# Gradients of a GELU layer: copies out of one PSUM tile put in the planned order, and the engines' orders written anew

## The chip, the cores and the metric

One core of one Trainium2 chip. The metric is the device time of one execution in microseconds; the span in the profile goes from the first to the last instruction. Engine names as in the profile: PE is TensorE (PEld its weight loads), DVE VectorE, ACT ScalarE, POOL GpSimd, SP SyncE, which here issues DMAs.

## The reference

A dense layer with tanh-GELU and a second dense layer, forward and backward. All inputs and outputs are bfloat16. S = 2048 rows, D = 448, F = 1792.

```python
h = jnp.einsum("bsd,df->bsf", x, w1) + b1
h = gelu(h)                                   # tanh form
out = jnp.einsum("bsf,fd->bsd", h, w2) + b2
# outputs: out, and the gradients of x, w1, b1, w2, b2 for a given grad_out
```

## The kernel before, in words

Every engine's program is a list written out by hand: `PE_ORDER`, `ACT_ORDER`, `DVE_ORDER`, `SP_ORDER`. A token names a step. A small planner (`Plan`) turns the tokens into operations. `emit` writes an operation out when everything that it needs has been written out, engine by engine in the order of the lists; the semaphores follow from the tiles that the written instructions share. So where two engines use one tile, the one written out first goes first, and the other waits.

The rows are worked in 4 blocks of 512. In each block the 1792 columns of the hidden layer go in 7 pairs of 128-column tiles, so there are 28 pairs, p = 0 to 27. The steps:

- PE: `W6`, `w4` are warm-up matmuls; `X0` to `X3` transpose four tiles of x for block 0; `B` spreads b2. `u p.d` is x times w1 for pair p, in two runs d = 1, 2, of 3 and 4 pairs of matmuls (d = 1 has 4 and d = 2 has 3 for p below 7). A pair of matmuls is two half-height matmuls side by side, into two PSUM banks. `h0.d` and `h1.d` are u for pair 0 in two halves of 256 columns: h0 needs x's tiles 0 and 1, h1 needs tiles 2 and 3. `q p.d` is grad_out times w2 transposed, into the tile `qb` (banks 6 and 7). `p p.i` are the units of the output in block 0, two pairs of matmuls each; `o b.half...` are units of the output of block b and `x b.half...` units of x's gradient, 4 or 6 pairs of matmuls each, into banks 0 to 3. After the last unit stand the gradients of w1 (L780) and of w2 (L834), 16 matmuls for each bank.
- u goes to banks 4 and 5 in general, but to 0 and 1 for p = 1 and to qb's two banks for p = 2 and p = 4 (`U_BANK`). Bank halves change sides between d = 1 and d = 2, and a run waits for a word from POOL (L235) where that is so.
- `c pA`, `c pB` copy u's two banks with b1 into a bf16 tile (L410 on ACT, L412 on DVE). `X0` to `X3` in the lists of ACT and DVE empty x's transposed tiles (L582). `b1T` transposes b1 in four small instructions (L675), and every c needs it. `b2c` empties B's bank.
- ACT: `g` GELU (L430), `s` square (L435), `t` tanh (L460). DVE: `e`, `r`, `y`, `z`, `m`, `n` (L440 to L470) work out the derivative, and `G` (L475) multiplies it with q out of qb. So q of pair p + 1 can start only when G of pair p is done.
- `vo b.j` empties a bank of the output with b2 (L496, always DVE), `vx b.j` a bank of x's gradient (L501 on ACT).
- SP: `L0` to `L3` load parts of w1, `Z0` to `Z2` its last 128 rows into `gh_nat`, `F` and `R` two more copies of 64 rows of w1, `K` parts of w2, `X`, `Y` transposing loads of x and grad_out, `J`, `I` transposed weights, `H`, `T` stores and transpositions of h and its gradient, `S` stores of output blocks, `Nx`, `Ng` loads for the last stage.

u of pair 2 wants L2 and Z1; u of pair 4 wants L3 and, with its fourth pair of matmuls, Z2.

In `C` (L395 on) stands the rule on copies out of qb. It acts only where B is on DVE and A on ACT, and no pair of this kernel is so: c2A is on DVE and c2B on ACT, and both c4 are on DVE.

Of the kernel before, what the change touches and what calls it, by code (L numbers as in the profile page):

```python
# [108 lines left out]
ACT_ORDER = """
xr12 L0 Z0 b2 table X1 X3 c0A0 c0A1 s0 g0 s1 g1 c2B t0 s2 g2 g3 s3 c5B g4 g5 t1 c6B t2 g6 s4 s5 g7 c8A c8B g8 c9A c9B  # L110
g9 c10A c10B t3 t4 g10 s6 c11A c11B s7 g11 t5 c12A c12B g12 s8 t6 c13A c13B g13 s9 t7 s10 c14A c14B t8 t9 g14 c15A s11
s12 c15B t10 g15 c16A s13 c16B t11 g16 vx0.0 vx0.1 s14 c17A c17B t12 vx0.2 vx0.3 g17 s15 c18A c18B t13 g18 s16 c19A
c19B t14 g19 t15 c20A s17 c20B g20 s18 t16 c21A c21B s19 t17 g21 c22A c22B g22 s20 t18 c23A c23B g23 s21 t19 s22 t20
s23 c24A c24B t21 vx1.0 vx1.1 vx1.2 vx1.3 g24 s24 c25A c25B t22 t23 g25 s25 c26A c26B s26 g26 t24 c27A c27B g27 s27
t25 vx2.0 vx2.1 vx2.2 vx2.3 t26 t27 vx3.0 vx3.1 vx3.2 vx3.3
"""
DVE_ORDER = """
ident X0 b1T X2 b2c c0B0 c0B1 c1A c1B e0 r0 y0 c2A c3A c3B z0 e1 m0 r1 n0 c4A c5A c4B z1 e2 y1 r2 y2 z2 c6A m1 n1 m2
n2 c7A c7B Dg0 G0 vo0.2 vo0.3 e3 r3 vo0.0 z3 vo0.1 G1 y3 e4 r4 y4 z4 m3 n3 m4 G2 n4 e5 r5 y5 z5 G3 m5 e6 n5 r6 y6 z6
G4 m6 e7 n6 r7 y7 z7 G5 m7 e8 vo1.0 r8 vo1.1 z8 vo1.2 vo1.3 G6 n7 e9 y8 r9 y9 z9 m8 G7 m9 n8 n9 e10 r10 y10 z10 G8 e11  # L120
m10 r11 n10 z11 y11 G9 m11 e12 n11 r12 y12 z12 G10 m12 e13 n12 r13 y13 z13 G11 e14 r14 m13 z14 n13 y14 G12 e15 r15 y15
m14 z15 n14 m15 G13 n15 e16 r16 y16 z16 G14 m16 e17 n16 r17 y17 z17 vo2.0 vo2.1 G15 m17 vo2.2 vo2.3 n17 e18 r18 y18
z18 G16 m18 e19 n18 r19 y19 z19 m19 G17 n19 e20 r20 y20 z20 G18 m20 e21 n20 r21 y21 z21 G19 e22 r22 m21 z22 n21 y22
G20 e23 r23 y23 z23 m22 n22 m23 G21 n23 e24 r24 y24 z24 m24 n24 G22 e25 r25 y25 z25 m25 G23 n25 e26 r26 y26 z26 m26
G24 n26 e27 r27 y27 z27 m27 n27 G25 vo3.0 vo3.1 G26 vo3.2 vo3.3 G27
"""
# [33 lines left out]
def make_plan(tc, ctx, x, w1, b1, w2, b2, grad_out, out_0, out_1, out_2, out_3, out_4, out_5):  # L160
# [239 lines left out]
    def C(p, h, eng, hf=None):  # L400
        ft = 2 * (p % NPB) + h
        v = val(("ub", p), F_UB[p])
        if hf is None:
# [4 lines left out]
        bias = b1T[:, ft:ft + 1]
        if eng == "ACT":
            fn = lambda: nc.scalar.activation(out=out, in_=src, func=ACT.Identity, bias=bias)  # L410
        else:
            fn = lambda: nc.vector.tensor_scalar(out=out, in0=src, scalar1=bias, scalar2=None, op0=ALU.add)  # L412
# [465 lines left out]
```

## Time and profile before

| | us |
|---|---|
| median of 3 runs | 266.11 (265.84 to 266.29) |
| the profiled execution | 266.0 |
| its span | 264.2 |
| PE busy | 259.6 |
| DVE busy | 196.2 |
| ACT busy | 131.5 |

A row of the timeline gives start, length, engine, line, operation, output from input, count, and in brackets the idle time ahead of it with what ended it. A row of the waits gives the total, the times and the longest. A row of a stage gives its ends, its length, then busy time and count of PE, PEld, DVE, ACT and POOL, the granted clock, the DMA engines' share and GB/s. A matmul's end is modelled, so its start is the firmer number. The granted TensorE clock is 1.00 throughout.

### The profile page before, as it was taken

What the parts mean: (1) busy time and instruction counts of PE and PEld (TensorE: products, weight loads), DVE (VectorE), ACT (ScalarE), POOL (GpSimd) and SP (SyncE); (2) the same over time, 40 slices, a digit from 0 to 9 for tenths busy, and PEclk for the clock granted to TensorE, in tenths of its full rate; (3) what the DMA queues carried; (4) which work ended last, traced back from release to release, by engine and by line L of the source; (5) the groups of instructions that cost most, each with busy time, mean ns of one, the idle gap of its engine ahead of it and who ended that gap; (6) DMA issues with size and microseconds to landing.
All of it is one profiled execution on the core that took longest, in us unless ns stands there. A gap on an engine that the chain in (4) does not pass through costs nothing.

```text
span 264.2 us, 5344 instructions
## 1 busy us (share of the span) xinstructions
PE 259.6 (98%) x2185; PEld 158.2 (60%) x2185; DVE 196.2 (74%) x279; ACT 131.5 (50%) x172; POOL 14.6 (6%) x12
## 2 busy tenths in 40 slices
PE   8989999999999999999999999999999999999996
PEld 4545555566666666677677777765555555555554
DVE  6699399899978899999996986379999996011000
ACT  4789749864889896973998430021112111000001
POOL 1000000000000000000000000000000872100000
PEclk9999999999999999999999999999999999999999
DMA  7999988999997965594557942895898999973221
GB/s 209 298 188 227 168 138 191 285 317 203 252 215 154 212 178 122 136 178 107 102 143 197 298 96 42 149 289 137 176 235 159 163 226 164 226 167 119 69 72 35
DMA packets 120107, 46.50 MB, mean 176 GB/s; under 512 B 96671, under 2 KB 119953, under 8 KB 120082
## 3 DMA queue, kind: packets, MB, share of 16 engines
q1 hardware_dynamic: 119392, 45.71, 79.1%
q10 hardware_dynamic: 690, 0.44, 0.5%
q8 instruction: 17, 0.28, 0.5%
q14 instruction: 8, 0.07, 0.1%
HBM read 8.09 MB, written 14.28 MB: 85 GB/s over the span
## 4 chain that ended last, share of the span: by engine, by line
PE 94%; ACT 2%; DVE 2%; DMA 1%; issue 0%; POOL 0%; DVEq 0%; ACTq 0%; POOLq 0%
PE bank L240 45%; PE qb L240 16%; PE bank L780 16%; PE bank L834 16%; DMA b1n<-in_b_dram 1%; ACT HG L430 1%; ACT TR L435 1%; DVE gh_nat L412 1%; DVE ub L412 0%; DVE b1T L675 0%; DVE xT L582 0%; ACT ub L410 0%; POOL st L667 0%; ACT w_sb L839 0%; POOL b1n L670 0%
## 5 line engine op out<-in xcount | busy, mean ns | idle before, releaser
L240 PEld LDWEIGHTS <-HG 64*128 64x128 bf16 x896 | 60.2, 94 | 27.8 <-POOLq L235 1.9
L240 PE MATMUL qb<-gT,w2Tf 64*128 64x512 bf16 x392 | 53.6, 376 | 0.0
L240 PE MATMUL bank<-w_sb,HG 64*128 64x448 bf16 x448 | 49.0, 349 | 0.0
L240 PE MATMUL bank<-xT,w1f 64*128 64x512 bf16 (+1 forms) x360 | 48.3, 370 | 0.7 <-DVE xT L582 0.4
L240 PE MATMUL bank<-w1T_sb,HG 64*128 64x448 bf16 x448 | 48.3, 349 | 0.0
L475 DVE SCALAR_TENSOR_TENSOR HG<-TR,qb 128x1024 bf16<-128x1024 bf16 x28 | 34.0, 1216 | 13.8 <-PE qb L240 13.8
L834 PE MATMUL bank<-w2Tf,HG 128*128 128x448 bf16 (+2 forms) x240 | 42.6, 340 | 0.0
L780 PE MATMUL bank<-w1f,gh_nat 128*128 128x448 bf16 x224 | 42.5, 352 | 0.0
L240 PEld LDWEIGHTS <-w2Tf 64*128 64x128 bf16 x392 | 26.4, 94 | 14.2 <-POOLq L235 0.3
L834 PEld LDWEIGHTS <-HG 128*128 128x128 bf16 x240 | 22.9, 98 | 19.8
L780 PEld LDWEIGHTS <-gh_nat 128*128 128x128 bf16 x224 | 21.8, 98 | 20.6 <-issue 0.4
L240 PEld LDWEIGHTS <-w1f 64*128 64x128 bf16 x382 | 23.6, 94 | 17.3 <-issue 1.3
L460 ACT ACTIVATE TR<-TR 128x1024 bf16<-128x1024 bf16 x28 | 29.3, 1054 | 8.4 <-DVE TR L450 8.1
L803 DVE TENSOR_TENSOR w1T_sb<-w1T_sb,gh_nat 128x1792 f32<-128x1792 f32 x14 | 28.4, 2026 | 0.5
L840 DVE CAST w_sb<-bank 128x448 bf16<-128x448 f32 x6 | 3.7, 624 | 29.7 <-PE bank L834 29.7
L785 ACT ACTIVATE TR<-bank 128x448 bf16<-128x448 f32 x14 | 7.6, 544 | 34.3 <-PE bank L780 34.3
L839 ACT CAST w_sb<-bank 128x448 bf16<-128x448 f32 (+2 forms) x9 | 4.4, 491 | 37.7 <-PE bank L834 37.7
L465 DVE TENSOR_SCALAR TR<-TR 128x2048 bf16<-128x2048 bf16 x28 | 19.2, 687 | 4.1 <-ACT TR L460 4.1
L809 POOL PARTITION_ALL_REDUCE w1T_sb<-w1T_sb x1 | 10.6, 10570 | 203.7 <-DVE w1T_sb L807 203.7
L470 DVE TENSOR_TENSOR TR<-TR 128x1024 bf16<-128x1024 bf16 x28 | 19.1, 685 | 0.2
L455 DVE TENSOR_TENSOR TR<-TR,HG 128x1024 bf16<-128x1024 bf16 x28 | 19.1, 683 | 0.0
L435 ACT ACTIVATE TR<-gh_nat 128x1024 bf16<-128x1024 bf16 x15 | 15.6, 1049 | 7.0 <-DVE TR L470 6.9
(51 smaller groups left out, 190.5 us busy)
## 6 DMA issues: line engine op xcount, KB each, us to landing
hT_dram<-HG SPq DMA_DIRECT2D x28, 256.0 KB, 3.9
out_dram<-st SPq DMA_DIRECT2D x16, 224.0 KB, 2.7
w1f<-in_x_dram SPq DMA_DIRECT2D x2, 896.0 KB, 8.1
w2Tf<-in_grad_out_dram SPq DMA_DIRECT2D x2, 560.0 KB
...
```

The costliest lines, as they stand in the source:

```text
L240: m = nc.tensor.matmul(bk_(b)[:, 0:n], lhsT=l, rhs=r, start=st, stop=sp, skip_group_check=True)
L435: pl.op("ACT", f"s{p}", lambda: nc.scalar.activation(out=TR[p % NTR][:, 1], in_=ubuf(p), func=ACT.Square, scale=sc), [("ub", p)], [v], ("a ...
L455: pl.op("DVE", f"R{p}", lambda: nc.vector.tensor_tensor(out=t[:, 1], in0=t[:, 1], in1=hblk(p), op=ALU.mult), [("r", p), ("h", p)], [val((" ...
L460: pl.op("ACT", f"t{p}", lambda: nc.scalar.activation(out=t[:, 0], in_=t[:, 0], func=ACT.Tanh), [("y", p)], [val(("t", p), ("TR0", p % NTR) ...
L465: pl.op("DVE", f"m{p}", lambda: nc.vector.tensor_scalar(out=t[:], in0=t[:], scalar1=1.0, scalar2=None, op0=ALU.subtract), [("t", p), ("r2" ...
L470: pl.op("DVE", f"n{p}", lambda: nc.vector.tensor_tensor(out=t[:, 0], in0=t[:, 0], in1=t[:, 1], op=ALU.mult), [("m0", p), ("m1", p)], [val( ...
L475: pl.op("DVE", f"G{p}", lambda: nc.vector.scalar_tensor_tensor(out=ghblk(p), in0=t[:, 0], scalar=2.0, in1=qb[:, :, :], op0=ALU.subtract, o ...
L780: nc.tensor.matmul(bk_(bk)[:, 0:D], lhsT=gh_nat[:, st // 4, ft, st % 4, :], rhs=x_nat[:, st, :], start=(st == 0), stop=(st == NS - 1))
L785: fn = (lambda dst=dst, src=src: nc.scalar.mul(out=dst, in_=src, mul=-0.5)) if eng == "ACT" else \
L803: nc.vector.tensor_tensor(out=hs3, in0=a, in1=gh_nat[:, st // 4, :, st % 4, :], op=ALU.add)
L809: pl.op("POOL", "gb1", lambda: nc.gpsimd.partition_all_reduce(gb1_w, hsum, channels=P, reduce_op=bass_isa.ReduceOp.add), ["hsc"], ["gb1"], ...
L834: nc.tensor.matmul(bk_(bk)[:, 0:d1 - d0], lhsT=h_nat[ft][:, st, :], rhs=g_nat[:, st, d0:d1], start=(st == 0), stop=(st == NS - 1))
```

## The change

One rule is widened and the four orders are written anew. The work is the same: the same matmuls, copies and loads.

```diff
-        if hf is None and u_banks(p)[0] == 6 and f"c{p}B" in DVE_ORDER.split() and f"c{p}A" in ACT_ORDER.split():
-            if eng == ("DVE" if p in ACT_FIRST else "ACT"):
-                after(o, [("u", p, 1 - h)])
+        other = DVE_ORDER if eng == "ACT" else ACT_ORDER
+        if hf is None and u_banks(p)[0] == 6 and f"c{p}{'BA'[h]}" in other.split() and eng == ("DVE" if p in ACT_FIRST else "ACT"):
+            after(o, [("u", p, 1 - h)])
```

`after` makes an operation be written out behind all readers of the named value: c2B on ACT is now written out after c2A on DVE.

The orders, cut to where they differ most:

```diff
 PE_ORDER
-... p0.0 p0.1 p0.2 p0.3 p1.0 u4.1 u5.1 u4.2 u5.2 p1.1
+... p0.0 p0.1 p0.2 p0.3 p1.0 p1.1 u4.1 u5.1 u4.2 u5.2
-... q6.2 x0.0.0.6.1 u14.1 x0.1.0.6.1 u14.2 q7.1 x0.0.0.6.2
-q7.2 u15.1 x0.1.0.6.2 u15.2 q8.1 x0.0.6.10.1 q8.2 x0.1.6.10.1 x0.0.6.10.2 u16.1 x0.1.6.10.2 u16.2 q9.1 x0.0.10.14.1
+... q6.2 x0.0.0.6.1 x0.1.0.6.1 u14.1 q7.1 u14.2 q7.2
+x0.0.0.6.2 x0.1.0.6.2 u15.1 q8.1 u15.2 q8.2 x0.0.6.10.1 x0.1.6.10.1 u16.1 q9.1 u16.2 q9.2 x0.0.6.10.2 u17.1
...
-... q18.1 x1.1.6.10.1 q18.2
-x1.0.6.10.2 x1.1.6.10.2 q19.1 x1.0.10.14.1 q19.2 ...
+... x1.0.0.6.2 q18.1 x1.1.0.6.2 q18.2 x1.0.6.10.1
+x1.1.6.10.1 q19.1 x1.0.6.10.2 q19.2 ...
...
-x2.0.0.6.1 x2.1.0.6.1 q21.1 u26.1 q21.2 u26.2 x2.0.0.6.2 x2.1.0.6.2 u27.1 x2.0.6.10.1 u27.2 x2.1.6.10.1 q22.1
+... q21.1 u26.1 q21.2 u26.2 x2.0.0.6.1 x2.1.0.6.1 x2.0.0.6.2 u27.1 x2.1.0.6.2 u27.2 q22.1 x2.0.6.10.1 q22.2
...
 ACT_ORDER
-... c2B t0 s2 g2 g3 s3 c5B g4 g5 t1 c6B t2 g6 s4 s5 g7 ...
+... c2B t0 s2 g2 g3 s3 c5B g4 t1 t2 c6B g5 g6 s4 s5 g7 ...
-... vx0.0 vx0.1 ... vx0.2 vx0.3 ... vx1.0 vx1.1 vx1.2 vx1.3 ... vx2.0 vx2.1 vx2.2 vx2.3 ... vx3.0 vx3.1 vx3.2 vx3.3
+... vx0.2 ... vx1.1 vx1.3 ... vx2.0 vx2.2 ... vx3.0 vx3.2
 DVE_ORDER
-ident X0 b1T X2 b2c c0B0 c0B1 c1A c1B e0 r0 y0 c2A c3A c3B z0 e1 m0 r1 n0 c4A c5A c4B z1 ...
+ident X0 X2 b1T c0B0 b2c c0B1 c1A c1B e0 r0 y0 c2A c3A c3B z0 e1 m0 r1 n0 z1 c4A c5A c4B ...
+... n12 z13 vx0.0 vx0.1 G11 vx0.3 ... G20 vx1.0 vx1.2 ... n25 vx2.1 vx2.3 ... G27 vx3.1 vx3.3
 SP_ORDER
-xr01 xr24 b1 L1 L2 Z1 K0 L3 K1 Z2 K2 F X1 K3 R Y0 J0 J1 Y1 J2 I0 E J3 I1 ...
+xr01 xr24 b1 L1 Z1 L2 K0 L3 K1 F Z2 K2 X1 K3 R Y0 J0 J1 J2 Y1 I0 E J3 I1 ...
```

The further steps of u, q, o and x, and the stores and transpositions on SP's queue, change places by a few steps in the same manner.

More of the change, by code (lines that the diff above doesn't have):

```diff
@@ L91 @@
 PE_ORDER = """
-W6 X0 X1 w4 X2 X3 h0.1 B h0.2 h1.1 u1.1 h1.2 u1.2 u2.1 u3.1 u2.2 u3.2 p0.0 p0.1 p0.2 p0.3 p1.0 u4.1 u5.1 u4.2 u5.2 p1.1
+W6 X0 X1 w4 X2 X3 h0.1 B h0.2 h1.1 u1.1 h1.2 u1.2 u2.1 u3.1 u2.2 u3.2 p0.0 p0.1 p0.2 p0.3 p1.0 p1.1 u4.1 u5.1 u4.2 u5.2
 p1.2 p1.3 p2.0 p2.1 p2.2 p2.3 u6.1 p3.0 u6.2 p3.1 p3.2 p3.3 p4.0 p4.1 u7.1 p4.2 u7.2 p4.3 p5.0 p5.1 p5.2 p5.3 u8.1
-p6.0 u8.2 q0.1 p6.1 q0.2 u9.1 p6.2 u9.2 q1.1 p6.3 q1.2 u10.1 o1.1.0.6.1 u10.2 q2.1 o1.0.0.6.1 u11.1 q2.2 u11.2
+p6.0 u8.2 q0.1 p6.1 q0.2 u9.1 p6.2 u9.2 q1.1 p6.3 q1.2 u10.1 o1.0.0.6.1 u10.2 q2.1 o1.1.0.6.1 u11.1 q2.2 u11.2
@@ L95 @@
 o1.0.0.6.2 o1.1.0.6.2 q3.1 u12.1 q3.2 u12.2 o1.0.6.10.1 q4.1 o1.1.6.10.1 u13.1 q4.2 u13.2 o1.0.6.10.2 q5.1 o1.1.6.10.2
-q5.2 o1.0.10.14.1 o1.1.10.14.1 o1.0.10.14.2 q6.1 o1.1.10.14.2 q6.2 x0.0.0.6.1 u14.1 x0.1.0.6.1 u14.2 q7.1 x0.0.0.6.2
-q7.2 u15.1 x0.1.0.6.2 u15.2 q8.1 x0.0.6.10.1 q8.2 x0.1.6.10.1 x0.0.6.10.2 u16.1 x0.1.6.10.2 u16.2 q9.1 x0.0.10.14.1
-q9.2 x0.1.10.14.1 u17.1 x0.0.10.14.2 u17.2 q10.1 x0.1.10.14.2 q10.2 o2.0.0.6.1 u18.1 q11.1 u18.2 q11.2 o2.1.0.6.1
-o2.0.0.6.2 u19.1 q12.1 u19.2 q12.2 o2.1.0.6.2 o2.0.6.10.1 u20.1 q13.1 u20.2 q13.2 o2.1.6.10.1 o2.0.6.10.2 o2.1.6.10.2
@@ L100 @@
-q14.1 o2.0.10.14.1 q14.2 u21.1 o2.1.10.14.1 u21.2 q15.1 o2.0.10.14.2 q15.2 u22.1 o2.1.10.14.2 u22.2 x1.0.0.6.1 q16.1
-u23.1 q16.2 u23.2 x1.1.0.6.1 x1.0.0.6.2 u24.1 q17.1 u24.2 q17.2 x1.1.0.6.2 x1.0.6.10.1 q18.1 x1.1.6.10.1 q18.2
-x1.0.6.10.2 x1.1.6.10.2 q19.1 x1.0.10.14.1 q19.2 x1.1.10.14.1 x1.0.10.14.2 x1.1.10.14.2 u25.1 q20.1 u25.2 q20.2
-x2.0.0.6.1 x2.1.0.6.1 q21.1 u26.1 q21.2 u26.2 x2.0.0.6.2 x2.1.0.6.2 u27.1 x2.0.6.10.1 u27.2 x2.1.6.10.1 q22.1
-x2.0.6.10.2 q22.2 x2.1.6.10.2 x2.0.10.14.1 x2.1.10.14.1 q23.1 x2.0.10.14.2 q23.2 x2.1.10.14.2 o3.0.0.6.1 q24.1
@@ L105 @@
-o3.1.0.6.1 q24.2 o3.0.0.6.2 o3.1.0.6.2 o3.0.6.10.1 o3.1.6.10.1 q25.1 o3.0.6.10.2 q25.2 o3.1.6.10.2 o3.0.10.14.1
-o3.1.10.14.1 q26.1 o3.0.10.14.2 q26.2 o3.1.10.14.2 x3.0.0.6.1 q27.1 x3.0.0.6.2 x3.1.0.6.1 q27.2 x3.1.0.6.2 x3.0.6.10.1
+q5.2 o1.0.10.14.1 o1.1.10.14.1 o1.0.10.14.2 q6.1 o1.1.10.14.2 q6.2 x0.0.0.6.1 x0.1.0.6.1 u14.1 q7.1 u14.2 q7.2
+x0.0.0.6.2 x0.1.0.6.2 u15.1 q8.1 u15.2 q8.2 x0.0.6.10.1 x0.1.6.10.1 u16.1 q9.1 u16.2 q9.2 x0.0.6.10.2 u17.1
+x0.1.6.10.2 u17.2 q10.1 x0.0.10.14.1 q10.2 u18.1 x0.1.10.14.1 u18.2 q11.1 x0.0.10.14.2 q11.2 u19.1 x0.1.10.14.2 u19.2
@@ new lines @@
+q12.1 o2.0.0.6.1 u20.1 q12.2 u20.2 o2.1.0.6.1 o2.0.0.6.2 q13.1 o2.1.0.6.2 q13.2 o2.0.6.10.1 o2.1.6.10.1 q14.1
+o2.0.6.10.2 q14.2 o2.1.6.10.2 o2.0.10.14.1 u21.1 q15.1 u21.2 q15.2 o2.1.10.14.1 o2.0.10.14.2 u22.1 q16.1 u22.2 q16.2
+o2.1.10.14.2 u23.1 x1.0.0.6.1 u23.2 x1.1.0.6.1 q17.1 u24.1 q17.2 u24.2 x1.0.0.6.2 q18.1 x1.1.0.6.2 q18.2 x1.0.6.10.1
+x1.1.6.10.1 q19.1 x1.0.6.10.2 q19.2 x1.1.6.10.2 x1.0.10.14.1 x1.1.10.14.1 u25.1 q20.1 u25.2 q20.2 x1.0.10.14.2
+x1.1.10.14.2 q21.1 u26.1 q21.2 u26.2 x2.0.0.6.1 x2.1.0.6.1 x2.0.0.6.2 u27.1 x2.1.0.6.2 u27.2 q22.1 x2.0.6.10.1 q22.2
@@ L107 @@
+x2.1.6.10.1 x2.0.6.10.2 x2.1.6.10.2 q23.1 x2.0.10.14.1 q23.2 x2.1.10.14.1 x2.0.10.14.2 x2.1.10.14.2 q24.1 o3.0.0.6.1
+q24.2 o3.1.0.6.1 o3.0.0.6.2 o3.1.0.6.2 q25.1 o3.0.6.10.1 q25.2 o3.1.6.10.1 o3.0.6.10.2 o3.1.6.10.2 q26.1 o3.0.10.14.1
+q26.2 o3.1.10.14.1 o3.0.10.14.2 o3.1.10.14.2 q27.1 x3.0.0.6.1 q27.2 x3.1.0.6.1 x3.0.0.6.2 x3.1.0.6.2 x3.0.6.10.1
 x3.1.6.10.1 x3.0.6.10.2 x3.1.6.10.2 x3.0.10.14.1 x3.1.10.14.1 x3.0.10.14.2 x3.1.10.14.2
@@ L109 @@
 ACT_ORDER = """
[L110 to L114, printed above, removed]
@@ L115 @@
-t25 vx2.0 vx2.1 vx2.2 vx2.3 t26 t27 vx3.0 vx3.1 vx3.2 vx3.3
+xr12 L0 Z0 b2 table X1 X3 c0A0 c0A1 s0 g0 s1 g1 c2B t0 s2 g2 g3 s3 c5B g4 t1 t2 c6B g5 g6 s4 s5 g7 c8A c8B g8 c9A c9B
+g9 c10A c10B t3 t4 g10 s6 c11A c11B s7 g11 t5 c12A c12B g12 s8 t6 c13A c13B g13 s9 t7 s10 t8 c14A c14B t9 g14 s11 s12
+c15A c15B t10 g15 c16A c16B s13 t11 g16 c17A c17B s14 t12 g17 c18A c18B s15 g18 vx0.2 c19A c19B t13 t14 g19 s16 c20A
+c20B s17 g20 t15 s18 t16 s19 c21A c21B t17 g21 c22A c22B s20 t18 g22 c23A c23B g23 s21 t19 s22 t20 s23 c24A c24B t21
@@ L116 @@
+g24 s24 c25A c25B vx1.1 vx1.3 t22 g25 t23 c26A c26B g26 s25 s26 t24 c27A c27B g27 s27 t25 vx2.0 vx2.2 t26 t27 vx3.0
+vx3.2
 """
 DVE_ORDER = """
-ident X0 b1T X2 b2c c0B0 c0B1 c1A c1B e0 r0 y0 c2A c3A c3B z0 e1 m0 r1 n0 c4A c5A c4B z1 e2 y1 r2 y2 z2 c6A m1 n1 m2
-n2 c7A c7B Dg0 G0 vo0.2 vo0.3 e3 r3 vo0.0 z3 vo0.1 G1 y3 e4 r4 y4 z4 m3 n3 m4 G2 n4 e5 r5 y5 z5 G3 m5 e6 n5 r6 y6 z6
-G4 m6 e7 n6 r7 y7 z7 G5 m7 e8 vo1.0 r8 vo1.1 z8 vo1.2 vo1.3 G6 n7 e9 y8 r9 y9 z9 m8 G7 m9 n8 n9 e10 r10 y10 z10 G8 e11
@@ L121 @@
[L121 to L125, printed above, removed]
+ident X0 X2 b1T c0B0 b2c c0B1 c1A c1B e0 r0 y0 c2A c3A c3B z0 e1 m0 r1 n0 z1 c4A c5A c4B e2 y1 r2 y2 z2 c6A m1 m2 n1 n2
@@ new lines @@
+c7A c7B Dg0 G0 vo0.2 vo0.3 e3 r3 vo0.0 vo0.1 z3 G1 y3 e4 r4 y4 z4 m3 n3 m4 G2 n4 e5 r5 y5 z5 G3 m5 e6 n5 r6 y6 z6 G4
+m6 e7 n6 r7 y7 z7 G5 m7 e8 vo1.0 r8 vo1.1 vo1.2 vo1.3 z8 G6 n7 e9 y8 r9 y9 z9 m8 G7 n8 m9 e10 n9 r10 y10 z10 G8 e11
+r11 m10 z11 n10 y11 G9 e12 r12 m11 z12 n11 y12 G10 e13 m12 r13 n12 z13 vx0.0 vx0.1 G11 vx0.3 e14 y13 r14 y14 z14 m13
+n13 m14 G12 n14 e15 r15 y15 z15 G13 m15 e16 n15 r16 y16 z16 G14 m16 e17 n16 r17 y17 z17 G15 vo2.0 vo2.1 m17 e18 n17
+r18 y18 z18 vo2.2 vo2.3 G16 m18 e19 n18 r19 y19 z19 G17 m19 e20 n19 r20 y20 z20 G18 m20 e21 n20 r21 y21 z21 G19 e22
@@ L126 @@
+r22 m21 z22 n21 y22 G20 vx1.0 vx1.2 e23 r23 y23 m22 z23 G21 m23 n22 n23 e24 r24 y24 z24 m24 n24 G22 e25 r25 y25 z25
+m25 G23 n25 vx2.1 vx2.3 e26 r26 y26 z26 G24 m26 e27 n26 r27 y27 z27 m27 n27 G25 G26 vo3.0 vo3.1 vo3.2 vo3.3 G27 vx3.1
+vx3.3
 """
 SP_ORDER = """
-xr01 xr24 b1 L1 L2 Z1 K0 L3 K1 Z2 K2 F X1 K3 R Y0 J0 J1 Y1 J2 I0 E J3 I1 So0.1 So0.0 X2 H0 H1 H2 H3 H4 H5 H6 H7 H8 H9
-T0 T1 H10 T2 H11 T3 H12 T4 H13 T5 So1.0 So1.1 T6 T7 H14 T8 H15 Y2 X3 T9 Sx0.0 H16 Sx0.1 T10 H17 T11 H18 T12 H19 T13
@@ L130 @@
-H20 T14 So2.0 T15 So2.1 H21 Y3 H22 T16 H23 T17 T18 T19 Sx1.0 Sx1.1 H24 T20 H25 T21 Nx H26 H27 T22 Sx2.0 Sx2.1 T23 T24
-T25 So3.0 T26 So3.1 Ng T27 Sx3.0 Sx3.1
+xr01 xr24 b1 L1 Z1 L2 K0 L3 K1 F Z2 K2 X1 K3 R Y0 J0 J1 J2 Y1 I0 E J3 I1 So0.1 So0.0 X2 H0 H1 H2 H3 H4 H5 H6 H7 H8 H9
+T0 T1 H10 T2 H11 T3 H12 T4 H13 T5 So1.0 So1.1 T6 T7 H14 T8 Y2 H15 T9 X3 H16 T10 H17 Sx0.0 Sx0.1 T11 H18 H19 T12 H20
+T13 T14 T15 So2.0 Y3 H21 So2.1 T16 H22 H23 T17 T18 T19 H24 Sx1.0 T20 Sx1.1 H25 T21 H26 Nx H27 T22 T23 Sx2.0 Sx2.1 T24
@@ L132 @@
+T25 T26 So3.0 So3.1 Ng T27 Sx3.0 Sx3.1
 """
```

## The prediction

> **What bounds the kernel now.** I read the page's engine line first, then the chain that ended last, then the busy time by stage, and last the timeline of TensorE around its stops.
>
> ```profile
> PE 259.6 (98%) x2185; PEld 158.2 (60%) x2185; DVE 196.2 (74%) x279; ACT 131.5 (50%) x172; POOL 14.6 (6%) x12
> ```
> ```profile
> 6.00 0.70 DVE xT L582
> ...
> 13.77 0.75 DVE ub L412
> 14.52 1.33 DVE gh_nat L412 x2
> ...
> 31.35 0.86 PE qb L240 x8
> ...
> 176.66 42.48 PE bank L780 x224
> 219.14 42.43 PE bank L834 x240
> ```
> ```profile
> 0.00:15.89 15.89, 13.95 (x125) 6.94 (x126) 10.63 (x27) 10.23 (x14) 1.16 (x10) 1.00 0.91 233
> 15.89:176.66 160.77, 160.77 (x1597) 106.61 (x1597) 136.77 (x218) 108.03 (x134) 0.00 (x0) 1.00 0.85 184
> ```
>
> TensorE (the column after the length of the stage) is busy for all of 160.77 us from 15.89 on, and then the chain is its two last groups of matmuls, 42.48 and 42.43 us, back to back. The order of steps changes but not one matmul is added or taken away, so from 15.89 on there is nothing to win. Only the first 15.89 us hold stops. They also hold the three pieces of VectorE in the chain above, which is where the change works. So I ask two things: how long are these stops, and does the new order keep the later 160 us free of them?
>
> A busy TensorE hides short stops, because the end of a matmul is modelled. I therefore measure from start to start.
>
> ```profile
> 5.80 0.50 PE L240 MATMUL bank<-xT,w1f 64*128 64x256 bf16 x5
> 6.75 0.50 PE L240 MATMUL bank<-xT,w1f 64*128 64x256 bf16 x6 [0.44 <-DVE xT L582]
> 7.19 0.81 PE L240 MATMUL bank<-xT,w1f 64*128 64x512 bf16 x6
> 12.05 2.06 PE L240 MATMUL bank<-w_sb,HG 64*128 64x448 bf16 x20
> 14.57 0.82 PE L240 MATMUL qb<-xT,w1f 64*128 64x512 bf16 x6 [0.46 <-DVE ub L412]
> 15.89 0.82 PE L240 MATMUL bank<-xT,w1f 64*128 64x512 bf16 x6 [0.28 <-DVE gh_nat L412]
> 18.05 2.83 PE L240 MATMUL bank<-w_sb,HG 64*128 64x448 bf16 x28
> ```
>
> Two halves run side by side, so I count pairs. h1.1 has four pairs of 256 columns and takes 7.19 - 6.75 = 0.44, 0.11 a pair. h0.2 has three, so it is done issuing at 5.80 + 0.33 = 6.13; h1.1 starts at 6.75. **First stop: 0.62.** The rows with 28 and 20 matmuls differ by four pairs and 2.83 - 2.06 = 0.77, so 0.19 a pair of 448 columns. The ten pairs from 12.05 (p0.0 to p1.0) are issued by 13.95; u4.1 starts at 14.57. **Second stop: 0.62.** Eight matmuls of 512 columns take 0.86 in the chain, so u4.1 is issued by 15.43; u5.1 starts at 15.89. **Third stop: 0.46.** Together 1.70 us.
>
> **x's third tile ahead of b1's transpositions.**
>
> ```profile
> 5.12 0.85 DVE L675 STREAM_TRANSPOSE b1T<-b1n 32x32 bf16<-32x32 bf16 x4 [0.45 <-DMA b1n<-in_b_dram]
> 5.18 0.59 ACT L582 CAST xT<-bank 128x512 bf16<-128x512 f32 x1 [0.19 <-PE bank L575]
> 6.00 0.69 DVE L582 CAST xT<-bank 128x512 bf16<-128x512 f32 x1
> ```
>
> h1.1 needs x's tiles 2 and 3. Tile 3 is emptied by ScalarE at 5.18 to 5.77. Tile 2's matmuls are issued before tile 3's, so its copy on VectorE can start by 5.1 and ends by 5.8. Both are ready before TensorE comes at 6.13, and the first stop goes whole: -0.62. What is late instead is b1T: it runs 5.8 to 6.65 and not 5.12 to 5.97. Its readers are the copies of h0 (c0B0 on VectorE, c0A0 on ScalarE). These free banks 4 and 5 for u3.1. From u1.1's start at 7.19, u1.1, h1.2, u1.2 and u2.1 take 0.86, 0.33, 0.65 and 0.86 by the pair, so u3.1 comes at 9.89 - 0.62 = 9.3; a half-size copy takes no more than the 0.75 of a full one in the chain and ends by 7.4. Cost 0; without that room it would be the 0.7 by which b1T is late.
>
> **Copies out of qb in the planned order.**
>
> ```profile
> 11.35 0.69 DVE L450 TENSOR_TENSOR TR<-TR,ub 128x1024 bf16<-128x1024 bf16 x1
> 13.07 0.67 ACT L410 ACTIVATE ub<-qb,b1T 128x512 bf16<-128x512 f32 x1
> 13.77 0.75 DVE L412 TENSOR_SCALAR ub<-qb,b1T 128x512 bf16<-128x512 f32 x1 [1.74 <-ACT ub L410]
> ```
>
> Both copies of u2 read the one tile qb. In the program before, ScalarE's c2B is written out first, and VectorE's c2A waits for it: 1.74 us with nothing done, and c3A and c3B stand behind it. Now c2A comes first and c2B waits. c2A can start at y0's end, 12.04, less the 0.62 by which the work ahead moves up: 11.4. By the chain c2A, c3A and c3B take 0.75 + 1.33 = 2.08, so c3B ends near 13.5. The added wait falls on ScalarE, where t0, s2, g2 and g3 are queued behind c2B. But c2A is done near 12.15, and ScalarE, busy with g1, comes to c2B only at 13.07 - 0.62 = 12.45, so the wait costs nothing. c2B ends at 13.1.
>
> u4.1 now stands behind p1.1, 0.38 of work more. It comes at 13.95 - 0.62 + 0.38 = 13.71, after c2A and c2B; u5.1 comes at 14.57, after c3B. Second and third stop go: -0.62 and -0.46. p1.1 is not lost, it is only done earlier. What is late next is c7B for u8.1.
>
> ```profile
> 26.60 1.40 DVE L412 TENSOR_SCALAR gh_nat<-bank,b1T 128x512 bf16<-128x512 f32 x2
> 28.25 0.83 PE L240 MATMUL bank<-xT,w1f 64*128 64x512 bf16 x6
> ```
>
> It has 0.25 us of room now and must come 1.70 earlier. VectorE enters this stretch 13.77 - 11.4 = 2.37 earlier with the same work, so it can.
>
> **Loads in another order on SP's queue.** Z1 goes ahead of L2 (both wanted by u2.1), F ahead of Z2 and K2.
>
> ```profile
> 5.74 0.49 SPq L516 DMA_DIRECT2D w_sb<-in_w_dram  x1
> 6.28 0.62 SPq L516 DMA_DIRECT2D gh_nat<-in_w_dram  x1
> 7.41 1.01 SPq L516 DMA_DIRECT2D w1f<-in_w_dram  x1
> 8.46 7.12 SPq L528 DMA_TRANSPOSE xT<-in_x_dram  x1
> ```
> ```profile
> w_sb<-in_w_dram SPq DMA_DIRECT2D x1, 224.0 KB, 6.6
> ```
> ```profile
> DMA packets 2034, 2.14 MB, mean 305 GB/s; under 512 B 192, under 2 KB 1999, under 8 KB 2034
> ```
>
> K1 (issued 5.74) lands 6.6 later, at 12.3; Z2 behind it has 192 KB, 0.64 us at the 305 GB/s of 6 to 13 us: an estimate of 13.0 to 13.3. F's 224 KB are now set whole ahead of it, 0.75 more: 13.8 to 14.1. u4.1 wants it with its fourth pair, 13.71 + 3 x 0.216 = 14.36. So cost 0, with 0.3 us of room where there was 1.9 (15.2 less 13.3). At worst Z2 lands with everything ahead of the transposing load, whose issue ends at 15.58: 1.2 lost. Nothing can be gained by it, as u4.1 didn't wait for Z2. K2 lands by 15.6 as well, and p2.0 wants it only near 17.5. [...] For L2, with Z1's 128 KB now ahead of it, I take 0, since the two end together as before, and 0.4 (128 KB at 305 GB/s) as the upper end. Y1 and J2 trade places too; q7.1 and q2.1 want them tens of microseconds later.
>
> **The middle: nine copies of x's gradient go from ScalarE to VectorE, q's steps move forward.** The costs of one copy (for VectorE the nearest row, a plain copy of the same size) and the tightest place:
>
> ```profile
> L501 ACT ACTIVATE st<-bank 128x448 bf16<-128x448 f32 x16 | 7.6, 549 | 19.0 <-PE bank L240 19.0
> L840 DVE CAST w_sb<-bank 128x448 bf16<-128x448 f32 x6 | 3.7, 624 | 29.7 <-PE bank L834 29.7
> ```
> ```profile
> 122.24 1.22 DVE L475 SCALAR_TENSOR_TENSOR HG<-TR,qb 128x1024 bf16<-128x1024 bf16 x1 [0.34 <-PE qb L240]
> 123.51 0.85 PE L240 MATMUL qb<-gT,w2Tf 64*128 64x512 bf16 x6
> ```
> ```profile
> 33.50:123.50 90.00, 90.00 (x888) 58.05 (x885) 83.12 (x137) 69.07 (x84) 0.00 (x0) 1.00 0.89 195
> ```
> ```profile
> DVE HG L475 <- PE qb L240: 4.8, 7, 1.4
> DVE TR L465 <- ACT TR L460: 1.5, 3, 0.8
> ```
>
> q19.1 follows G18's end (123.46) by 0.05. Up to there VectorE gets three copies more (vx0.0, vx0.1, vx0.3), 3 x 0.62 = 1.9. And between q18.2 and q19.1 stand two units of x1 where there were four, so q19.1 comes 2 x 0.76 = 1.5 earlier against the rest. So VectorE must take 3.4 us out of its idle time, which is 90.00 - 83.12 = 6.9. Of this 4.8 is waiting for q itself (the seven waits on qb), and q8 to q18 move forward too, so those waits shrink as they should. Half is needed and more than two thirds are of the kind that gives way: I take cost 0, with 0 to 3.4 as its bounds. Behind q21 four units of x2 and the whole of u27 stand ahead of q22.1, and VectorE has room again. The stores and transpositions on SP's queue are reordered here as well; none of VectorE's waits in this stretch is for a DMA, so I set them at 0.
>
> **The sum:** 0.62 + 0.62 + 0.46 = 1.70 less, nothing more. The profiled execution has 266.0 (span 264.2 and 1.8 around it), so 264.3. The median of the runs, 266.11, lies 0.1 above it: **264.4 us**.
>
> **The rivals.**
>
> Z2 or L2 late (F ahead): the stop at u4.1 comes back in part. For it: the queues are full until 13 us. Against it: 0.3 us of room by the estimate. It gives 264.4 and 0.3 to 1.2 more, 264.7 to 265.6.
>
> VectorE falls behind in the middle: q9.1 to q19.1 then wait for G, which waits for tanh and for the copies. It decides where VectorE turns less than 1.7 of the 3.4 us into work: then more is lost than the start gains. If none gives way, the kernel loses 3.4 less the 0.05 of room and gains 1.7: 266.1 + 1.65 = 267.7, slower. For it: VectorE is busy 92% there, and a copy costs it 0.62 where ScalarE takes 0.55. Against it: that idle time is mostly waiting for q. [...]
>
> The change doesn't do what it says: ScalarE, not VectorE, sets the start. When X2 and c2A are early, g0 and g1 hold p0.0 and p1.0 instead, because b1T, later by 0.7, holds ScalarE's c0A0. Then the shift is eaten before u4.1 and the time stays at 266.1. Against it: c0A1, which waits for h1.2 and so moves with TensorE, stands between c0A0 and g0.
>
> **How the numbers follow.** Forecast 0.62 (264.1 to 264.9, the upper end with 0.5 of small stops); late load 0.14; nothing left 0.07 (265.7 to 266.5, as the runs scatter by 0.45); VectorE behind 0.17 (266.7 to 267.7). About 0.2%, 0.53 us, is what a measurement of this kernel can tell from no change, so faster is under 265.6: the first two, 0.76. Same 0.07, slower 0.17. The range runs from 264.0 over the first two and most of the third: 266.1.
>
> **What the profile after would show.** Right: TensorE's starts of h1.1, u4.1 and u5.1 near 6.15, 13.7 and 14.6; ScalarE's c2B behind VectorE's c2A, no wait of 1.7 us on VectorE near 12; the first matmul of L780 near 175.0 and not 176.66. Wrong: a wait of the PE or PEld rows on a DMA near 14.4 (Z2), on DVE's HG between 60 and 125 us (G late), or stops on ScalarE's HG before 13 us.

## The result, and the profile after

| | before | after |
|---|---|---|
| median of the runs, us | 266.08 (265.84 to 266.29, 6 runs) | 265.10 (264.52 to 265.47, 6 runs) |
| the profiled execution, us | 266.0 | 265.37 |
| its span, us | 264.2 | 263.6 |

The ratio is 0.9963 (0.9950 to 0.9977): 0.98 us faster, where 1.70 was forecast. The profiled execution of the changed kernel is one of its slower ones. Line numbers are one higher in it (L241 for L240).

The shares of the chain in the kernel before; then the engine line and the chain's shares in the changed one:

```profile
PE 94%; ACT 2%; DVE 2%; DMA 1%; issue 0%; POOL 0%; DVEq 0%; ACTq 0%; POOLq 0%
```
```profile
PE 259.7 (99%) x2185; PEld 157.4 (60%) x2185; DVE 200.6 (76%) x288; ACT 127.1 (48%) x163; POOL 14.6 (6%) x12
...
PE 90%; SPq 5%; DMA 3%; issue 0%; ACTq 0%; ACT 0%
```

VectorE and ScalarE had 2% each and are gone from the chain. In their place stand SP's queue and the DMAs, 8% together. So the old waits went and loads took over at the start. The timeline of TensorE there:

```profile
4.58 0.66 PE L576 MATMUL bank<-st,TR 128*128 128x128 bf16 x8
...
6.23 0.49 PE L241 MATMUL bank<-xT,w1f 64*128 64x256 bf16 x6
...
8.84 0.82 PE L241 MATMUL qb<-xT,w1f 64*128 64x512 bf16 x6 [0.17 <-DMA w1f<-in_w_dram]
...
11.87 2.76 PE L241 MATMUL bank<-w_sb,HG 64*128 64x448 bf16 x24
14.45 0.83 PE L241 MATMUL qb<-xT,w1f 64*128 64x512 bf16 x6
...
15.31 0.83 PE L241 MATMUL bank<-xT,w1f 64*128 64x512 bf16 x6
...
23.11 0.93 PE L241 MATMUL bank<-w_sb,HG 64*128 64x448 bf16 x8 [0.16 <-DMA w_sb<-in_w_dram]
```

The three old stops are gone: h1.1 (6.23), u4.1 (14.45) and u5.1 (15.31) follow the work ahead of them without a gap and without a bracket. Three new ones are there, again counted from start to start. u2.1 at 8.84 is 0.34 late: it waits for L2, whose last piece landed at 8.79. In the row at 11.87 the twelve pairs need 12 x 0.189 = 2.27 and take 14.45 - 11.87 = 2.58: p1.0 (13.70) stood 0.31 for K1, landed at 13.65. p4.0 at 23.11 is 0.34 late for K3. That is 0.99 given back. h0.1 itself starts at 5.17, 0.09 later than before. 1.70 - 0.99 - 0.09 = 0.62, and the stages show it:

```profile
0.00:15.89 15.89, 14.81 (x135) 7.86 (x137) 12.90 (x31) 10.76 (x14) 1.16 (x10) 1.00 1.05 226
15.89:176.05 160.16, 160.00 (x1591) 104.85 (x1586) 135.12 (x221) 103.82 (x126) 0.00 (x0) 1.00 0.86 187
```
```profile
176.05 42.48 PE bank L781 x224
218.53 42.43 PE bank L835 x240
```

The two last groups begin at 176.05, 0.61 before the 176.66 of the kernel before, and take the same 42.48 and 42.43. Why K3 was late is read in the chain of waits:

```profile
8.12 9.31 SPq L529
17.44 0.05 issue
17.49 5.58 DMA w_sb<-in_w_dram
23.07 0.04 issue
23.11 0.91 PE bank L241 x7
```

The issue of the transposing load X1 (L529) holds SP's queue to 17.43, where it ended at 15.58 before. K3 stands behind it and lands at 23.07, 2.2 later than the 20.82 of before. This comes of one execution and not plainly of the order: in the three others with F ahead (e2, e6 and e8 below) the issue ends at 15.79 to 16.07 and K3 lands at 21.1 to 21.8, and in e4, with the old order, these are 16.09 and 22.0. The packet records of the execution shown have one thing more. The last six pieces of the loads ahead of X1 moved at 16.31 to 16.9, and none moved from 15.27 to 16.31, while one 16 KB packet of instructions went (15.26 to 16.33). That it held those pieces up fits these times; no run here shows it.

### The profile page after: what moved, and what is told of

Read it like the earlier page. It is cut to its first block, busy times and chain, and to the rows that moved or that the text cites. A ratio compares the mean times of both kernels' runs of the same rounds, so it can differ in the third digit from the quotient of the medians.

```text
span 263.6 us, 5352 instructions
## 1 busy us (share of the span) xinstructions
PE 259.7 (99%) x2185; PEld 157.4 (60%) x2185; DVE 200.6 (76%) x288; ACT 127.1 (48%) x163; POOL 14.6 (6%) x12
## 4 chain that ended last, share of the span: by engine, by line
PE 90%; SPq 5%; DMA 3%; issue 0%; ACTq 0%; ACT 0%
PE bank L241 42%; PE bank L781 16%; PE bank L835 16%; PE qb L241 16%; SPq L529 4%; DMA w_sb<-in_w_dram 2%; DMA w1f<-in_w_dram 1%; SPq L517 1%; ACTq L517 0%; ACT w_sb L840 0%
## 5 line engine op out<-in xcount | busy, mean ns | idle before, releaser
L241 PEld LDWEIGHTS <-HG 64*128 64x128 bf16 x896 | 59.6, 94 | 28.9 <-POOLq L236 1.5
L241 PE MATMUL qb<-gT,w2Tf 64*128 64x512 bf16 x392 | 53.5, 376 | 0.0
L241 PE MATMUL bank<-w_sb,HG 64*128 64x448 bf16 x448 | 49.1, 349 | 0.3 <-DMA w_sb<-in_w_dram 0.2
L241 PE MATMUL bank<-xT,w1f 64*128 64x512 bf16 (+1 forms) x360 | 48.1, 370 | 0.0
L241 PE MATMUL bank<-w1T_sb,HG 64*128 64x448 bf16 x448 | 47.5, 349 | 0.0
L476 DVE SCALAR_TENSOR_TENSOR HG<-TR,qb 128x1024 bf16<-128x1024 bf16 x28 | 34.1, 1216 | 12.7 <-PE qb L241 12.6
L241 PEld LDWEIGHTS <-w2Tf 64*128 64x128 bf16 x392 | 26.0, 94 | 14.7 <-POOLq L236 0.3
L781 PEld LDWEIGHTS <-gh_nat 128*128 128x128 bf16 x224 | 21.8, 98 | 20.6 <-issue 0.4
L241 PEld LDWEIGHTS <-w1f 64*128 64x128 bf16 x382 | 23.5, 94 | 16.2 <-POOLq L236 1.0
```

The source lines that it names most:

```text
L241: m = nc.tensor.matmul(bk_(b)[:, 0:n], lhsT=l, rhs=r, start=st, stop=sp, skip_group_check=True)
L476: pl.op("DVE", f"G{p}", lambda: nc.vector.scalar_tensor_tensor(out=ghblk(p), in0=t[:, 0], scalar=2.0, in1=qb[:, :, :], op0=ALU.subtract, o ...
L781: nc.tensor.matmul(bk_(bk)[:, 0:D], lhsT=gh_nat[:, st // 4, ft, st % 4, :], rhs=x_nat[:, st, :], start=(st == 0), stop=(st == NS - 1))
```

## The experiments

Each was measured beside the kernel before on the same chip; its medians there were 266.20, 266.04 and 266.03 us for the three groups of runs. Ratios are against those. The groups are told by what they separate.

**The load order taken out of the change (e1).**

```diff
 SP_ORDER
-xr01 xr24 b1 L1 Z1 L2 K0 L3 K1 F Z2 K2 X1 K3 R Y0 J0 J1 J2 Y1 ...
+xr01 xr24 b1 L1 L2 Z1 K0 L3 K1 Z2 K2 F X1 K3 R Y0 J0 J1 Y1 J2 ...
```

> The changed kernel with the first loads on SP's queue back in the order of before (L2 ahead of Z1, Z2 and K2 ahead of F, Y1 ahead of J2); all else as changed. Theory L (the new order of loads makes L2, K1 and, through the transposing load, K3 late; three stops of 0.34, 0.31 and 0.34 us come from that alone): L2 lands near 7.9, K1 near 12.3, K3 near 20.8 as before, no stop at u2.1, p1.0 and p4.0, L780 starts near 175.0, time 264.1 to 264.4. Theory N (the loads are slower because TensorE and the others work earlier, or by the chance of one execution; the order has no part in it): K1 near 13.6, transposing load's issue ends near 17.4, time near 265.1.

Measured: 264.67 (264.20 to 265.07), ratio 0.9944 (0.9932 to 0.9957). TensorE's timeline in it:

```profile
4.29 0.61 PE L576 MATMUL bank<-st,TR 128*128 128x128 bf16 x8
4.89 0.50 PE L241 MATMUL bank<-xT,w1f 64*128 64x256 bf16 x6
...
6.07 0.49 PE L241 MATMUL bank<-xT,w1f 64*128 64x256 bf16 x6
...
8.35 0.81 PE L241 MATMUL qb<-xT,w1f 64*128 64x512 bf16 x6
...
13.64 0.81 PE L241 MATMUL qb<-xT,w1f 64*128 64x512 bf16 x6
```

No matmul row waits for a load. u2.1 comes at 8.35, u4.1 at 13.64 (the prediction had 13.71), and p4.0 does not wait either. Of the three new stops, that of u2.1 comes back in every profiled execution with Z1 ahead (below); those of p1.0 and p4.0 were seen in one. The price of the order by the medians is 0.3 to 0.4 us (e8 and the change against e1), and the intervals overlap. The stops went as the first of the two expectations has it, but the median lies 0.3 above the 264.1 to 264.4 that it gave.

**The load order alone (e2)**, put into the kernel before.

```diff
 SP_ORDER
-xr01 xr24 b1 L1 L2 Z1 K0 L3 K1 Z2 K2 F X1 ...
+xr01 xr24 b1 L1 Z1 L2 K0 L3 K1 F Z2 K2 X1 ...
```

> The kernel of before with only the first loads on SP's queue in the new order. Theory L: K1 lands near 13.6 and K3 near 23, the transposing load's issue ends near 17.4 instead of 15.6; TensorE comes later here, so at most 0.1 to 0.3 us is lost: 266.1 to 266.4. Theory N: loads land as before (15.6, K3 20.8), time 266.1.

Measured: 266.03 (265.88 to 266.33), ratio 0.9997 (0.9988 to 1.0006). TensorE and then VectorE in its timeline:

```profile
9.57 0.82 PE L240 MATMUL qb<-xT,w1f 64*128 64x512 bf16 x6 [0.49 <-DMA w1f<-in_w_dram]
...
15.77 0.82 PE L240 MATMUL bank<-xT,w1f 64*128 64x512 bf16 x6 [0.25 <-DVE gh_nat L412]
```
```profile
13.65 0.75 DVE L412 TENSOR_SCALAR ub<-qb,b1T 128x512 bf16<-128x512 f32 x1 [1.73 <-ACT ub L410]
```

u2.1 is late here as well, by 0.66, and the kernel is not slower. VectorE's c2A still ends at 14.4 (14.5 before), so the time lost at u2.1 is taken from the stop that u4.1 would have had; that one is gone, and u5.1 still stops for 0.42. So the loss of 0.1 to 0.3 that was expected did not come. The late load costs nothing while the copies out of qb set the time; once they do not, nothing behind it takes the stop up.

**The rule alone (e3), and the rule with VectorE's new start (e4).**

```diff
+        other = DVE_ORDER if eng == "ACT" else ACT_ORDER
+        if hf is None and u_banks(p)[0] == 6 and f"c{p}{'BA'[h]}" in other.split() and eng == ("DVE" if p in ACT_FIRST else "ACT"):
+            after(o, [("u", p, 1 - h)])
 DVE_ORDER (e4 only)
-ident X0 b1T X2 b2c c0B0 c0B1 ...
+ident X0 X2 b1T c0B0 b2c c0B1 ...
```

> The kernel of before with only the widened rule on copies out of qb; every order as before, so u4.1 still stands ahead of p1.1. By the prediction's own steps the second and third stop go and the first stays: 1.08 us less, 265.0; u4.1 starts near 13.95. If u4.1's place behind p1.1 were needed, u4.1 would still stop for c2B (ends 13.7) or u5.1 for c3B (14.1), by 0.1 to 0.3: 265.1 to 265.3. If theory N holds, a stop on a load shows at u4.1 or p4.0 too, 265.3 or more.

> As the last, and x's third tile emptied ahead of b1's transpositions (the start of VectorE's list as changed); the orders of TensorE, ScalarE and SP and the rest of VectorE's as before. Prediction's steps: all three stops go, 1.70 us less, 264.4; so the new middle and the new loads bring nothing. Theory N: stops on loads of up to 1 us come in, 264.7 to 265.4. If q, G and the copies of the middle were too tight when all comes 1.7 earlier, a stop would show between 30 and 125 us.

Measured: e3 264.75 (264.73 to 264.93), ratio 0.9948 (0.9936 to 0.9961); e4 264.74 (264.49 to 265.20), ratio 0.9949 (0.9935 to 0.9962). TensorE in e3:

```profile
4.59 1.04 PE L575 MATMUL bank<-st,TR 128*128 128x128 bf16 x8
...
11.92 2.06 PE L240 MATMUL bank<-w_sb,HG 64*128 64x448 bf16 x20
13.81 0.81 PE L240 MATMUL qb<-xT,w1f 64*128 64x512 bf16 x6
...
14.68 0.81 PE L240 MATMUL bank<-xT,w1f 64*128 64x512 bf16 x6
```

Three widened lines are worth 1.45 us by the medians (1.08 was expected of e3). From h1.1 to u5.1 it was 15.89 - 6.75 = 9.14 us and is 14.68 - 6.62 = 8.06 in e3: 1.08 less, as summed. Both later stops go, and no step of TensorE had to be moved for it: p1.1 stands behind u5.2 as in the kernel before, and u4.1 still comes without a gap (11.92 + 10 x 0.189 = 13.81). So the forward move of p1.1, which the prediction counted as what gives the copies time, was not needed. e1 holds e4's two parts with p1.1's move and the new middle besides, and gives the same (264.67 against 264.74): these together are worth nothing that is seen here, in either direction. e4 has what the prediction counted 1.70 for; it came out 0.34 above the 264.4 expected of it, and no faster than e3: by these two medians x's third tile is worth 0.01.

In e4's profiled execution h0.1 started at 5.55 for another reason: a tile of x landed late.

```profile
4.99 0.62 PE L575 MATMUL bank<-st,TR 128*128 128x128 bf16 x8 [0.58 <-DMA TR<-in_x_dram]
```

**x's third tile: alone in the kernel before (e10), and taken back out of e1 (e9).** The edit of e10 is that of `DVE_ORDER` above without the rule; e9 undoes it in e1:

```diff
-ident X0 X2 b1T c0B0 b2c c0B1 ...
+ident X0 b1T X2 b2c c0B0 c0B1 ...
```

> The kernel of before with x's third tile emptied ahead of b1's transpositions as the only edit. The stop before u4.1 stays, as c2A still waits for c2B, and all of it moves with the start. Theory S: 0 to 0.6 earlier, on average 0.2 to 0.3, so 265.8 to 266.0 with a wider scatter than before. Theory of the prediction: 265.5. If c2B's place on ScalarE doesn't move with the start: 266.1.

> The changed kernel with the old order of its first loads, and x's third tile again behind b1's transpositions (b2c ahead of c0B0); all else as changed. With x's third tile first this kernel has 264.67 and runs from 264.2 to 265.07. Theory S (h1.1 then waits for X2 only where TensorE's start is early; h0.1 comes between 4.9 and 5.6 us as its clock is released and x's tiles land, and X2 ends near 6.7): slower by 0 to 0.6, on average 0.2 to 0.3, so 264.8 to 265.0, and a narrow scatter, since the start is pinned at 6.7. Theory of the prediction (first stop of 0.62 in every execution): 265.3.

Measured: e10 265.86 (265.35 to 266.31), ratio 0.9995 (0.9986 to 1.0004); e9 265.05 (264.79 to 265.17), ratio 0.9962 (0.9949 to 0.9974). TensorE in e10, its fastest execution; then TensorE and VectorE in e9:

```profile
6.12 0.49 PE L240 MATMUL bank<-xT,w1f 64*128 64x256 bf16 x6
...
13.94 0.82 PE L240 MATMUL qb<-xT,w1f 64*128 64x512 bf16 x6 [0.46 <-DVE ub L412]
...
15.26 0.83 PE L240 MATMUL bank<-xT,w1f 64*128 64x512 bf16 x6 [0.28 <-DVE gh_nat L412]
```
```profile
4.58 1.06 PE L576 MATMUL bank<-st,TR 128*128 128x128 bf16 x8
...
6.92 0.49 PE L241 MATMUL bank<-xT,w1f 64*128 64x256 bf16 x6
```
```profile
6.01 0.69 DVE L583 CAST xT<-bank 128x512 bf16<-128x512 f32 x1
```

In the execution that e10 shows, the first stop is gone whole: h1.1 at 6.12 and not 6.75, u4.1 and u5.1 each 0.63 earlier with their stops as they were. So the 0.62 is real for one execution. By the medians it is worth 0.17 alone (within what can be told from no change), and 0.4 by e9 against e1 (265.05 and 264.67; 0.5 by their ratios, as they were measured in different groups; the intervals overlap). A part of e9's lateness is no matter of x's third tile: in the execution shown the weight loads of h0.1 waited 0.40 for `gh_nat` (Z0), and h1.1 found X2 ready. The reason for the small worth lies a step further forward. h0.1 starts between 4.89 (e1) and 5.58 (e2) from one profiled execution to another, with the same steps ahead of it. With b1T first, X2 ends at 6.69 in before, 6.55 in e3 and 6.70 in e9, though TensorE starts h0.1 there at 5.08, 5.56 and 5.57, because b1 lands near 5.0 (b1T starts at 4.97 to 5.13) and the two instructions take 0.85 and 0.69. Where TensorE starts at 5.08, as in the profile before, it stops 0.62 for X2; where it starts at 5.56, as in e3 and e9, h1.1 is due at 6.6 or later and stops for nothing. The early start is what X2 ahead makes use of. Of the twelve profiled executions seven have h1.1 due by 6.3, with 0.5 to 0.7 to win against 6.75, and five at 6.6 or later, with 0.14 at most: 0.38 on average, an estimate from these starts. The scatter agrees in the main: with b1T first the times of a kernel in one group lie within 0.20 (e3) to 0.67 us (the kernel before beside e6 to e8), with X2 first within 0.51 (e6) to 0.96 (e10).

**Which of the moved loads (e6, e7), and the change once more beside them (e8).** Both start from e1; e6 sets F ahead again (and J2 ahead of Y1), e7 sets Z1 ahead again. e8 is the changed kernel itself.

```diff
 SP_ORDER of e6
-xr01 xr24 b1 L1 L2 Z1 K0 L3 K1 Z2 K2 F X1 ... Y1 J2 ...
+xr01 xr24 b1 L1 L2 Z1 K0 L3 K1 F Z2 K2 X1 ... J2 Y1 ...
 SP_ORDER of e7
-xr01 xr24 b1 L1 L2 Z1 K0 ...
+xr01 xr24 b1 L1 Z1 L2 K0 ...
```

> The changed kernel with the old order of its first loads, but F ahead of Z2 and K2 (and J2 ahead of Y1) as in the change. Theory F (F's load of 64 partitions slows the loads that share the engines with it): GB/s between 11 and 13 us fall from 320-350 to 225-240, K1 lands near 13.7 and the transposing load's issue ends after 16; stops at p1.0 and p4.0 (0.3 each when TensorE comes early), none at u2.1; time 264.9 to 265.1. Theory Z (Z1 ahead of L2 does the harm, F none): 321 GB/s and more, K1 near 12, time 264.67 as with the old order.

> The changed kernel with the old order of its first loads, but Z1 ahead of L2 as in the change. Theory F: L2 lands near 8.5 and u2.1 stops for it by up to 0.3 us where TensorE comes early, K1 near 12, no stop at p1.0 and p4.0; time 264.7 to 264.9. Theory Z: K1 near 13.7, stops at p1.0 and p4.0, 265.0 or more.

> The changed kernel as it is, beside the others on one chip. Both theories: near 265.1, 0.4 above the old order of loads, and a wide scatter (0.9 us), since stops on loads come and go with the moment at which TensorE's clock is released (4.66 us in its profile, 3.9 to 5.5 in others).

Measured: e6 264.70 (264.59 to 265.10), ratio 0.9951 (0.9939 to 0.9963); e7 264.96 (264.67 to 265.62), ratio 0.9959 (0.9947 to 0.9971); e8 264.96 (264.36 to 265.16), ratio 0.9953 (0.9941 to 0.9964). u2.1 in e7 and in e8:

```profile
9.32 0.82 PE L241 MATMUL qb<-xT,w1f 64*128 64x512 bf16 x6 [0.61 <-DMA w1f<-in_w_dram]
```
```profile
9.10 0.82 PE L241 MATMUL qb<-xT,w1f 64*128 64x512 bf16 x6 [0.45 <-DMA w1f<-in_w_dram]
```

In all four profiled executions with Z1 ahead u2.1 waits for L2: 0.34 (the change), 0.61 (e8), 0.66 (e2), 0.78 (e7), with L2 landing at 8.79 to 9.52. In the eight with the old order it lands at 7.54 to 8.54, and one of them shows a stop, of 0.25 (e5). So it is Z1 ahead of L2 that makes u2.1 stop. The time agrees, 264.96 for e7 and 264.67 and 264.70 for e1 and e6, but the ranges of these overlap, and so do the intervals: the stop is shown by the profiles, its 0.3 us by the medians only suggested.

F ahead costs nothing by e6's median. It does go with slower loads. The windows of e1, of e6 and of the change, with GB/s last:

```profile
9.00:11.00 2.00, 2.00 (x22) 0.93 (x20) 1.97 (x5) 2.00 (x3) 0.00 (x0) 1.00 1.05 376
11.00:13.00 2.00, 2.00 (x24) 0.95 (x22) 2.00 (x4) 2.00 (x4) 0.00 (x0) 1.00 1.21 324
```
```profile
9.00:11.00 2.00, 2.00 (x22) 0.92 (x20) 1.94 (x4) 1.79 (x3) 0.00 (x0) 1.00 1.00 313
11.00:13.00 2.00, 2.00 (x24) 0.93 (x20) 1.97 (x5) 2.00 (x3) 0.00 (x0) 1.00 1.07 237
```
```profile
9.00:11.00 2.00, 2.00 (x20) 0.88 (x18) 1.97 (x5) 2.00 (x3) 0.00 (x0) 1.00 1.03 314
11.00:13.00 2.00, 2.00 (x22) 0.97 (x20) 2.00 (x4) 2.00 (x3) 0.00 (x0) 1.00 1.08 224
```

From 11 to 13 us the four executions with F ahead move 224 to 237 GB/s and the eight others 307 to 374, about a third less. From 9 to 11 us the two kinds are not apart: 303 to 317 against 259 (before) to 376. K1, which is issued ahead of F, lands at 13.4 to 13.7 in the four executions that have F ahead and at 11.3 to 12.3 in the others. p1.0 wants it at 13.39 when TensorE is early, as in the change's profile, and later otherwise (13.64 in e8); so this stop comes in some executions alone. So neither expectation of e6 held whole: its loads slow as the one says, its median is that of the other. In e7 p1.0 and p4.0 do not stop.

**K3 ahead of the transposing load (e5)**, a trial of a better version on top of e1.

```diff
 SP_ORDER
-... K1 Z2 K2 F X1 K3 R ...
+... K1 Z2 K2 K3 X1 F R ...
```

> The changed kernel with the old order of its first loads, K3 moved ahead of the transposing load X1 and F behind it. If the last load that TensorE runs into is K3 (landed at 19.6 to 22.0 with the old order, wanted by p4.0 near 22.1 to 22.6): K3 lands near 17, X1 near 20 where u7.1 wants it at 22.6, no stop is left and the time is 264.3 to 264.5 with less scatter. If what scatters is only TensorE's start (clock release, x's first tiles): 264.67, as with the old order of loads.

Measured: 264.64 (264.44 to 265.20), ratio 0.9949 (0.9938 to 0.9961). No gain over e1, so K3 is not what holds e1. That its executions differ by the start of TensorE fits the profiles and is not shown run by run. The best of all is e1 and those beside it; between e1, e3, e4, e5 and e6 (264.64 to 264.75) these runs show no difference. The rule's three lines alone are as good as the whole change without its loads.

## Why the prediction was right, and where it was not

The direction, the range and the mechanism held: the time was won where three stops stood, and nothing was lost in the middle. The forecast's own case (264.1 to 264.9) did not hold the median of 265.10. That lies in the range of the rival of the late loads (264.7 to 265.6), and a late load, L2, is what the profiles show. That it still lies so near is in part luck: by the medians the rule brought more than was summed, x's third tile less, and the loads took some back.

**Copies out of qb: right in its working, and in the profiles in its size.** VectorE and ScalarE in the changed kernel:

```profile
11.43 0.75 DVE L413 TENSOR_SCALAR ub<-qb,b1T 128x512 bf16<-128x512 f32 x1
12.10 1.40 DVE L413 TENSOR_SCALAR gh_nat<-bank,b1T 128x512 bf16<-128x512 f32 x2
```
```profile
12.54 0.67 ACT L411 ACTIVATE ub<-qb,b1T 128x512 bf16<-128x512 f32 x1
```

c2A at 11.43 (11.4 was said), c3B's end at 13.50 (13.5), c2B at 12.54 and without a wait (12.45). The 1.74 us of idle VectorE is gone. Alone this was worth 1.26 by the two profiled executions (266.0 and 264.74), of which 0.13 is a h1.1 that started earlier; from there to u5.1 it is the 1.08 that was summed. The 1.45 of the medians has 0.2 more, as the kernel before had 266.20 in that group; where that lies no profile shows.

**x's third tile: right in one execution, over-sized for the median.** The term was 0.62 and measured 0.01 (e4 against e3), 0.17 (e10) and 0.4 to 0.5 (e9 against e1), none of them clear of the noise. The failing step is that the stop was read from one execution, in which TensorE started early, and carried over to the median as if every execution had it. The sentence that the median lies 0.1 above the profiled execution hid it: with b1T first h1.1 comes at 6.75 where TensorE starts at 5.08 (before) and at 6.64 where it starts at 5.58 (e2), so the times agree though the starts do not.

**Loads: the step that failed is the cost 0 of L2.** "The two end together as before, and 0.4 as the upper end": L2 landed at 8.8 to 9.5 where the old order has 7.5 to 8.5, and the stop was 0.34 to 0.78. The prediction looked closely at Z2, which did not stop u4.1 anywhere: by the change's trace it landed at 14.72 where 13.8 to 14.1 was estimated, and was wanted at 14.45 + 0.65 = 15.1. K2 landed at 17.48, where "by 15.6" was said, and no row stopped for it. K1 and K3 weren't looked at, since both are issued on the same side of the moved loads as before; K1 still landed some 1.4 us later with F ahead (13.36 in e6, 11.98 in e1). K3 was 2.2 later in the execution shown; that this is F's doing is not shown. The transposing load's issue was watched as a bound for Z2 alone. Z2 did land later with F ahead, at 14.6 to 15.0 in the four executions against 12.7 to 13.3 in before, e1 and e4; that it comes later by just the 0.75 of F's bytes was the author's estimate. Why K1 is later with F issued behind it, no run here shows.

**The middle: right, cost 0.** A window that begins at the prediction's step and ends 0.9 us behind q19.1's start, its waits, and the tight place:

```profile
32.90:122.30 89.40, 89.40 (x882) 57.33 (x880) 85.39 (x142) 67.11 (x81) 0.00 (x0) 1.00 0.91 200
```
```profile
DVE HG L476 <- PE qb L241: 3.1, 6, 1.1
```
```profile
120.11 1.22 DVE L476 SCALAR_TENSOR_TENSOR HG<-TR,qb 128x1024 bf16<-128x1024 bf16 x1 [0.35 <-PE qb L241]
...
121.39 0.85 PE L241 MATMUL qb<-gT,w2Tf 64*128 64x512 bf16 x6
```
```profile
L504 DVE TENSOR_SCALAR st<-bank 128x448 bf16<-128x448 f32 x9 | 5.3, 617 | 7.6 <-PE bank L241 7.4
L502 ACT ACTIVATE st<-bank 128x448 bf16<-128x448 f32 x7 | 3.7, 544 | 22.2 <-PE bank L241 22.2
```

VectorE's idle time fell from 6.9 to 89.40 - 85.39 = 4.0 (the same 4.0 up to q19.1's start, 88.50 - 84.49), and its waits for q from 4.8 to 3.1. TensorE is busy for all 89.40. q19.1 still starts right behind G18 (120.11 + 1.22 = 121.33, then 121.39). So the rival with VectorE behind fell: VectorE gave 2.9 us of its idle time, where 3.4 was estimated, and 4.0 are left. A copy is 0.073 us dearer on VectorE (617 and 544 ns). Nine of them cost nothing that is seen here, since neither engine sets the time there. The rival that ScalarE holds the start fell too: p0.0 starts at 11.87 without a gap, and p1.0 waited for K1.

**What is open.** L2 lands some 1.1 later with 128 KB of Z1 ahead of it (the middle of four executions against the middle of eight). Its later issue makes 0.3 of that and the bytes at 305 GB/s 0.4, an estimate; the rest is not explained. The same holds for the lower rate with F ahead: in the packet records the 1536-byte pieces of the other loads take up to 120 ns (90th percentile) in the changed kernel and 65 in e1. F's pieces go to 64 partitions and not to 128, and at 3584 bytes they are larger; no run here changed either alone. Against F as such stands e1: from 12.0 to 12.5 thirty of F's pieces moved there, and the 896-byte pieces beside them kept their 41 ns.
